# Streaming attention heads tiled by 55 queries over one 128-row key window each

## The chip, the core and the metric

The kernel runs on one core of a Trainium2 chip. The core has a matrix engine (TensorE, "PE" in the profile, with its weight loads as "PEld"), a vector engine (DVE), an activation engine (ACT), a general engine (POOL, which also issues software-described DMAs) and a queue engine (SP, which here issues plain and transposing DMAs). The metric is the device time of one execution in microseconds (us); lower is better.

## The reference, cut to what matters

Attention over 4 batches, 8 heads, 768 positions and head size 64, followed by a mixture of 4 experts over the 3072 rows of 512. Heads 0, 2 and 6 ("retrieval") attend to every earlier position. Heads 1, 3, 4, 5 and 7 ("streaming") see only the first 4 positions (the sinks) and the last 64.

```python
pos = np.arange(S)                        # S = 768
rel = pos[:, None] - pos[None, :]
causal = rel >= 0
is_sink = pos[None, :] < 4
in_win = (rel >= 0) & (rel < 64)
stream_keep = causal & (is_sink | in_win)
mask = np.where(retr, causal, stream_keep)            # per head
a = softmax(np.where(mask, q @ k.T / 8, -1e9))
x = (a @ v), heads side by side                       # (3072, 512)
...
for e in range(4):
    h = np.maximum(x @ w1[e], 0.0)                    # 512 -> 1024
    out += p[:, e:e+1] * (h @ w2[e])                  # 1024 -> 512
```

## The kernel before

**Groups.** The 768 positions of a batch are two chunks of 384 (`CH`), so there are eight groups `g` of (batch b, chunk c). The attention of a group makes `xT[g]`; `moe_group(g)` runs the four experts over its 384 rows. After the attention of group 0, the loop at the end runs `moe_group(g)` and, woven into it, `attention` of group g+1. Both are generators: a step of the expert work is four first-layer matmuls of 384 columns (line 648, then a relu on ACT into `hs`, line 661) or four second-layer matmuls of 512 columns (line 669). After each, attention steps are drawn until their nominal time has the share of `att_ns` that the expert work has of its stretch. So the order on every engine is fixed in the program[...].

**A head.** `scores` multiplies key tiles with the transposed queries into a bank of `pA` (four banks in all, shared with the first expert layer), takes the exp on ACT (line 499), and multiplies by a 0/1 mask on DVE (line 503) where the tile has an edge. `values` multiplies the value tiles with these into `pV` (two banks). A value tile of 128 columns holds the 64 of the head in one half and constants in the other, so that the same matmul gives the sum of the weights; ACT turns it into a reciprocal (Ln on line 548, Exp of the negative on line 558), and DVE scales (line 553). Heads interleave: `scores(h)` with `values(h-1)`.

**Tiles of a streaming head.** A key tile has 96 positions (`TK`) in its rows 32 to 127 and copies of the four sinks in rows 0 to 3. The 96 keys are visible to 160 queries (`TQ`), their own 96 and the next 64. A chunk therefore takes four tiles of 160, 160, 160 and 96 query columns, and chunk 1 also 64 columns of the last tile of chunk 0. `score_tiles` lists this: two banks and two masks a head.

**Data.** For groups 2 and later, POOL issues the loads two groups ahead (`load_k`, `load_q`, `load_v`), casting from float32 to float16. Keys and queries go to row-major buffers: `kRr` and `kSr` (one for each chunk), and `q16`. `dma_transposes`, issued from SP halfway through a group, copies the sinks into `kSr`, then transposes `q16`, `kRr` and `kSr` into `qT`, `kR` and `kS`. Values need no transposing; `sink_rows` copies their sinks. `kS` and `vS` exist twice, by the parity of the batch. Batch 0 is prepared on PE and DVE instead.

Of the kernel before, what the change touches and what calls it, by code (L numbers as in the profile page):

```python
# [10 lines left out]
FP16 = mybir.dt.float16  # L11
AF = mybir.ActivationFunctionType
ALU = mybir.AluOpType
# [4 lines left out]
def kernel(  # L18
# [21 lines left out]

    nc = tc.nc
    P = 128
    B, H, S, D = q.shape
# [19 lines left out]
    NT = S // TK  # L65
    TC = CH // TK
    assert NS <= R0 and NW == 64 and NS + NW <= TK

    pers = ctx.enter_context(tc.tile_pool(name="pers", bufs=1))
    att = ctx.enter_context(tc.tile_pool(name="att", bufs=1))  # L70
# [16 lines left out]
    w2sb = pers.tile([P, E * FTP, DM], FP16, name="w2sb")  # L87
    NR, NSH = len(RH), len(SH)
    kR = []
    kS = []  # L90
    vR = []
    vS = []
    for i in range(2):
        kR.append(pers.tile([P, NCH, NR, 3, P], FP16, name=f"kR{i}"))
        kS.append(pers.tile([P, NCH, TC, NSH, P], FP16, name=f"kS{i}"))
        vR.append(pers.tile([P, S // P, len(RH), P], FP16, name=f"vR{i}"))
        vS.append(pers.tile([P, NT, len(SH), P], FP16, name=f"vS{i}"))

    ident32 = pers.tile([P, P], FP32, name="ident32")
    ident16 = pers.tile([P, P], FP16, name="ident16")  # L100
# [3 lines left out]
    eps = pers.tile([P, 1], FP32, name="eps")  # L104
    mC = pers.tile([P, 2 * P], FP16, name="mC")
    mS = pers.tile([P, 4, TQ], FP16, name="mS")
    probs = pers.tile([P, NTILE, E], FP32, name="probs")
    psums = pers.tile([P, NTILE], FP32, name="psums")
    rprobs = pers.tile([P, NTILE], FP32, name="rprobs")
    p_sb = pers.tile([P, NTILE, E], FP32, name="p_sb")  # L110


    kRr = [pers.tile([P, NR, 3, P], FP16, name=f"kRr{c}") for c in range(NCH)]
    kSr = [pers.tile([P, TC, NSH, P], FP16, name=f"kSr{c}") for c in range(NCH)]


    def own(h):
        u = h % 2
        return slice(u * D, (u + 1) * D)

    def key_tile(b, h, t):

        i = b % 2
        if RETR[h]:
            return kR[i][:, t // 3, RH.index(h), t % 3, :]
        return kS[i][:, t // TC, t % TC, SH.index(h), :]

    def v_tile(b, h):

        i = b % 2  # L130
        if RETR[h]:
            return vR[i][:, :, RH.index(h), :]
        return vS[i][:, :, SH.index(h), :]


    q16 = {}
# [3 lines left out]

    def tiles_of(x, b, h, c):
        return x[b, h, c * CH : (c + 1) * CH, :].rearrange("(t r) d -> r t d", r=TK)

    def load_by_rows(x, x16, b, c):
        for j in range(3):
# [19 lines left out]
    def load_k(b, c):  # L165

        for h in range(H):
            if RETR[h]:
                gp.dma_start(  # L169
                    out=kRr[c][:, RH.index(h), :, own(h)], in_=rows_of(k, b, h, c)  # L170
                )
            else:
                gp.dma_start(  # L173
                    out=kSr[c][R0:P, :, SH.index(h), own(h)], in_=tiles_of(k, b, h, c)
                )

    qTs = {}
# [1 line left out]
    def alloc_qT(b, c):  # L179
        qTs[b, c] = att.tile([P, HP, CH], FP16, name="qT", bufs=2)  # L180

    def dma_transposes(b, c):
        i = b % 2
        first = kSr[0][R0 : R0 + NS, 0:1, :, :].rearrange("p t s x -> p t (s x)")
        nc.sync.dma_start(
            out=kSr[c][0:NS, :, :, :].rearrange("p t s x -> p t (s x)"),
            in_=first.to_broadcast([NS, TC, NSH * P]),
        )
        alloc_qT(b, c)
        for j in range(3):  # L190
            nc.sync.dma_start(
                out=qTs[b, c][:, :, j * P : (j + 1) * P],
                in_=q16[b, c][:, j, :, :].rearrange("p h d -> p (h d)"),
                transpose=True,
            )
        for x, xr in ((kR, kRr), (kS, kSr)):
            nc.sync.dma_start(
                out=x[i][:, c, :, :, :].rearrange("p t s x -> p (t s) x"),
                in_=xr[c].rearrange("p t s x -> p (t s x)"),
                transpose=True,  # L200
            )

    def load_v(b, c, heads):
        for h in heads:
            t = v_tile(b, h)
            if RETR[h]:
                gp.dma_start(  # L207
                    out=t[:, 3 * c : 3 * c + 3, own(h)], in_=rows_of(v, b, h, c)
                )
            else:  # L210
                gp.dma_start(  # L211
                    out=t[R0:P, TC * c : TC * (c + 1), own(h)],
                    in_=tiles_of(v, b, h, c),
                )

    def sink_row(b, h, c):
        t = v_tile(b, h)[:, :, own(h)]
        nc.vector.tensor_copy(  # L218
            out=t[0:NS, TC * c : TC * (c + 1), :],
            in_=t[R0 : R0 + NS, 0:1, :].to_broadcast([NS, TC, D]),  # L220
        )

    def sink_rows(b, c):
        x = vS[b % 2].rearrange("p t s x -> p t (s x)")
        nc.sync.dma_start(
            out=x[0:NS, TC * c : TC * (c + 1), :],
            in_=x[R0 : R0 + NS, 0:1, :].to_broadcast([NS, TC, NSH * P]),
        )
# [30 lines left out]
    def zero(eng, t):  # L259
        fill(eng, t.rearrange("p a b x -> p (a b x)"), 0.0)  # L260

    def one_values(eng, i, c):

        t = slice(3 * c, 3 * c + 3)
        fill(eng, vR[i][:, t, :, D:P], ONES)
        t = slice(TC * c, TC * (c + 1))
        fill(eng, vS[i][0:R0, t, :, :].rearrange("p t h x -> p t (h x)"), ONES)
        fill(eng, vS[i][:, t, 0:2, 0:D], ONES)
        fill(eng, vS[i][:, t, 2, D:P], ONES)
        fill(eng, vS[i][:, t, 3:5, 0:D], ONES)  # L270

    assert all(h % 2 == 0 for h in RH) and [h % 2 for h in SH] == [1, 1, 0, 1, 1]

# [18 lines left out]
    nc.vector.memset(eps, 1e-9)  # L292
    nc.vector.memset(ones, ONES)
    make_identity(nc, ident32)
    one_values(nc.vector, 0, 0)
    load_v(0, 0, [0, 1, 2, 3])
    zero(nc.vector, kR[0][:, 0, :, :, :])
    zero(nc.vector, kS[0][:, 0, :, :, :])
    nc.vector.tensor_copy(out=ident16, in_=ident32)


# [21 lines left out]
    def mask_s(x, n, keep, drop):  # L323
# [14 lines left out]
            fill=drop, base=-NW, pattern=[[1, TK]], channel_multiplier=-1,  # L338
        )

    mask_c(bC, 0.0, -60000.0)
    mask_s(bS, 3, 0.0, -60000.0)
    load_v(0, 0, [4, 5, 6, 7])
# [4 lines left out]
    load_triples(q, qt16, 0, 1)  # L348
    load_w2(0)
    zero(gp, kR[0][:, 1, :, :, :])  # L350
    zero(gp, kS[0][:, 1, :, :, :])
    one_values(gp, 0, 1)
    load_v(0, 1, range(5))
    load_w1(1, 0, F)
    load_v(0, 1, range(5, H))
# [3 lines left out]
        load_w2(e)  # L359
    mSf = mS.rearrange("p t x -> p (t x)")  # L360
    bSf = bS.rearrange("p t x -> p (t x)")


    xT = {}
# [4 lines left out]
    def attention(b, c):  # L369
# [5 lines left out]
        def transposes(hp):  # L375
            for x, is_k in ((k32 if first else k16, 1), (q32 if first else qt16, 0)):
# [20 lines left out]
                for u in range(2):  # L397
                    h = 2 * hp + u
                    r = slice(u * D, (u + 1) * D)
                    if RETR[h]:  # L400
                        nc.vector.tensor_copy(  # L401
                            out=rows_in_order(
                                kR[i][r, c, RH.index(h), :, :].rearrange(
                                    "r t x -> r (t x)"
                                )
                            ),
                            in_=cols(ps[r, :]),
                        )
                        continue
                    n = SH.index(h)  # L410
                    x_in, x_out = ps[r, 0:CH], kS[i][r, c, :, n, R0:P]
                    if first:
                        x_in = x_in.rearrange("r (t x) -> r t x", x=TK)
                    else:
                        x_in = x_in.rearrange("r (j t p) -> r j t p", j=3, t=TC)
                        x_out = x_out.rearrange("r t (p j) -> r j t p", j=3)
                    nc.vector.tensor_copy(out=x_out, in_=x_in)  # L417
                    sinks = kS[i][r, c, :, n, 0:NS]
                    if c == 0:
                        sink_k[h] = pers.tile([P, NS], FP16, name=f"sk{h}")  # L420
                        nc.vector.tensor_copy(out=sink_k[h][r, :], in_=ps[r, 0:NS])
                        src, op = ps[r, 0:NS], nc.vector.tensor_copy
                    else:
                        src, op = sink_k[h][r, :], nc.scalar.copy
                    src = src.rearrange("r (o x) -> r o x", o=1)
                    op(out=sinks, in_=src.to_broadcast([D, TC, NS]))
# [11 lines left out]
        def score_tiles(h):  # L438
            if RETR[h]:
                if c == 0:  # L440
# [7 lines left out]
                    (512, [(0, 0, 256, 128), (1, 128, 0, 384)], []),  # L448
                    (384, [(2, 0, 0, 384)], []),
                ]  # L450
            if c == 0:
                return [
                    (320, [(0, 0, 0, 160), (1, 160, 96, 160)], [(mSf, 0, 0, 320)]),
                    (256, [(2, 0, 192, 160), (3, 160, 288, 96)], [(mSf, 160, 0, 256)]),
                ]
# [18 lines left out]
        def scores(h):  # L474
            hp = h // 2
            es_of[h] = []
            for cols, parts, masks in score_tiles(h):
                ps = bank()
                ns = 0
                for n, (t, o, q0, nq) in enumerate(parts):  # L480
                    nc.tensor.matmul(  # L481
                        out=ps[:, o : o + nq],
                        lhsT=key_tile(b, h, t),
                        rhs=qTs[b, c][:, hp, q0 : q0 + nq],
                        start=(n == 0 or not first),
                        stop=not first,
# [26 lines left out]
        def values(h):  # L513
# [14 lines left out]
            for n, (es, t, o, q0, nq) in enumerate(work):  # L528
                nc.tensor.matmul(  # L529
                    out=ps[:, q0 : q0 + nq],  # L530
                    lhsT=v_tile(b, h)[:, t, :],
                    rhs=es[:, o : o + nq],
                    start=(n == 0),
                    stop=(n == len(work) - 1),
# [160 lines left out]
    for _ in attention(0, 0):  # L695
        pass

    for c in range(NCH):
        zero(gp, kRr[c])
        zero(gp, kSr[c])  # L700

    UNIT = FTP * DMP * mm_ns(CH) + 3 * FTP * mm_ns(DM)
    for g in range(G):
# [4 lines left out]
        if g + 2 < G:  # L708
            b2, c2 = divmod(g + 2, NCH)
            load_k(b2, c2)  # L710
            load_q(b2, c2)
            if b2 == 1:
                one_values(gp, b2, c2)
            load_v(b2, c2, range(H))

        begin = {0: 0.2, 1: 1.0}.get(g, 0.0) * UNIT
        end = {0: 2.2}.get(g, 0.93 * E) * UNIT

        att_ns = 4500.0 if nxt % NCH == 0 else 7700.0
        if nxt < NCH:  # L720
            att_ns += 8 * 3 * mm_ns(P)
        spent = 0.0
        done = 0.0
        to_transpose = g + 2 < G
# [47 lines left out]
```

The softmax here doesn't subtract the row's maximum and nothing guards it: scores larger than these inputs give would overflow.

## Time and profile before

The median of three runs is 417.66 us (417.56 to 418.54); the profiled execution spans 415.6 us.

| group of instructions | count | busy us | mean ns |
|---|---|---|---|
| PE first expert layer, 384 columns, L648 | 1024 | 187.7 | 326 |
| PE second expert layer, 512 columns, L669 | 768 | 180.7 | 379 |
| PE scores of streaming heads, 64 to 160 columns, L481 | 180 | 23.7 | 223 |
| PE scores of retrieval heads, 128 to 384 columns, L481 | 120 | 25.3 | 281 |
| ACT relu, L661 | 256 | 121.3 | 493 |
| ACT exp of scores, L499 | 152 | 71.6 | 481 |
| DVE masks of streaming heads, L503 | 70 | 22.2 | 317 |
| POOL issue of streaming key loads, L173 | 30 | 20.9 | 700 |
| POOL issue of streaming value loads, L211 | 40 | 28.1 | 706 |

Busy time is the time in which at least one instruction of the group was in flight. Matmuls are pipelined: each lasts longer than the distance to the next, so the mean duration of one isn't its cost. The granted clock of PE was 0.996 of full. DMA traffic is dense for the first third of the span and thin after it: in 40 slices, tenths of busy time were

```text
DMA  9999999999994700069963600046001000020002
```

### The profile page before, as it was taken

How to read it: one execution, taken by the hardware profiler on the slowest of the kernel's cores; microseconds unless marked ns; L12 is line 12 of the kernel's file. 1: busy time of each engine (PE TensorE's matmuls, PEld its weight loads, DVE VectorE, ACT ScalarE, POOL GpSimd, SP SyncE). 2: the span in 40 equal slices, each digit the busy share in tenths (PEclk: the TensorE clock that was granted, in tenths of full speed). 3: DMA queues.
4: the chain of work that ended last, by engine and by line, in shares of the span. 5: the costliest groups of instructions: out<-in, count | busy, mean ns of one | idle time of the engine just before them, and what ended most of it. 6: DMA issues, size and time to landing. Idle time of an engine off the chain costs nothing.

```text
span 415.6 us, 6541 instructions
## 1 busy us (share of the span) xinstructions
PE 401.6 (97%) x2520; PEld 228.3 (55%) x2520; DVE 163.3 (39%) x332; ACT 249.3 (60%) x539; POOL 120.2 (29%) x176
## 2 busy tenths in 40 slices
PE   7899999999999999999999999999999999999996
PEld 4665554555555555555555555555555555555552
DVE  7976553224432335333433333234443233432222
ACT  2676874337775657666764558666665577653331
POOL 8938319897980000039930000000000000000000
PEclk9899999999999999999999999999999999999999
DMA  9999999999994700069963600046001000020002
GB/s 173 146 196 204 209 205 109 177 182 146 88 91 118 98 1 2 25 126 164 83 39 94 117 2 2 0 107 105 2 0 61 18 2 0 2 76 2 0 0 76
DMA packets 117554, 33.70 MB, mean 81 GB/s; under 512 B 108100, under 2 KB 112404, under 8 KB 117524
## 3 DMA queue, kind: packets, MB, share of 16 engines
q0 software_dynamic: 71872, 17.05, 45.8%
q1 hardware_dynamic: 42452, 15.46, 18.1%
q10 hardware_dynamic: 3200, 0.79, 0.9%
q8 instruction: 19, 0.31, 0.3%
q14 instruction: 11, 0.09, 0.1%
HBM read 35.70 MB, written 6.29 MB: 101 GB/s over the span
## 4 chain that ended last, share of the span: by engine, by line
PE 86%; ACT 6%; DVE 4%; issue 1%; DMA 1%; ACTq 0%; DVEq 0%
PE pO L669 39%; PE pA L648 35%; PE pV L529 5%; PE pA L481 5%; ACT hs L661 2%; ACT rc L548 2%; DVE kS L417 1%; DMA q<-in_q_dram 1%; DVE vS L218 1%; ACT es L499 1%; ACT rc L558 1%; DVE kR L401 1%; ACTq L279 0%; DVE qT L392 0%; DVE es L503 0%
## 5 line engine op out<-in xcount | busy, mean ns | idle before, releaser
L648 PE MATMUL pA<-xT,w1sb 128*128 128x384 f16 x1024 | 187.7, 326 | 1.5 <-DVE kS L417 1.0
L669 PE MATMUL pO<-w2sb,hs 128*128 128x512 f16 x768 | 180.7, 379 | 0.0
L661 ACT ACTIVATE hs<-pA 128x384 f16<-128x384 f32 x256 | 121.3, 493 | 80.0 <-PE pA L648 73.4
L648 PEld LDWEIGHTS <-w1sb 128*128 128x128 f16 x1024 | 97.3, 98 | 59.7 <-issue 1.8
L669 PEld LDWEIGHTS <-hs 128*128 128x128 f16 x768 | 72.8, 98 | 72.7 <-ACT hs L661 0.5
L499 ACT ACTIVATE es<-pA 128x256 f16<-128x256 f32 (+3 forms) x152 | 71.6, 481 | 32.5 <-PE pA L481 29.5
L685 DVE SCALAR_TENSOR_TENSOR acc<-pO,p_sb,acc 128x512 f32<-128x512 f32 x72 | 54.0, 750 | 85.3 <-PE pO L669 84.8
L503 DVE TENSOR_TENSOR es<-es,mS 128x384 f16<-128x384 f16 (+1 forms) x70 | 22.2, 317 | 85.4 <-ACT es L499 85.0
L548 ACT ACTIVATE rc<-pV,eps 64x384 f32<-64x384 f32 x60 | 34.5, 575 | 34.7 <-PE pV L529 33.9
L173 POOL DMA_DIRECT2D kSr<-in_k_dram x30 | 20.9, 700 | 54.9 <-DMA kSr<-kSr 42.1
L553 DVE TENSOR_TENSOR xT<-pV,rc 64x384 f16<-64x384 f32 x60 | 33.1, 552 | 4.1 <-PE pA L648 1.7
L681 DVE TENSOR_SCALAR acc<-pO,p_sb 128x512 f32<-128x512 f32 x24 | 18.0, 750 | 37.7 <-PE pO L669 36.8
L558 ACT ACTIVATE rc<-rc 64x384 f32<-64x384 f32 x58 | 30.2, 522 | 1.8
L211 POOL DMA_DIRECT2D vS<-in_v_dram x40 | 28.1, 706 | 2.9 <-DMA q<-in_q_dram 2.2
L481 PE MATMUL pA<-qT,kS 128*128 128x160 f16 (+2 forms) x180 | 23.7, 223 | 3.4 <-ACT es L499 1.8
L481 PE MATMUL pA<-qT,kR 128*128 128x384 f16 (+2 forms) x120 | 25.3, 281 | 0.0
L481 PEld LDWEIGHTS <-kS 128*128 128x128 f16 x180 | 15.9, 98 | 15.2 <-issue 4.5
L503 DVE TENSOR_TENSOR es<-es,mC 128x256 f16<-128x256 f16 (+1 forms) x42 | 10.8, 256 | 29.4 <-ACT es L499 29.0
L529 PE MATMUL pV<-es,vR 128*128 128x384 f16 (+2 forms) x120 | 21.9, 281 | 0.0
L169 POOL DMA_DIRECT2D kRr<-in_k_dram x18 | 13.5, 751 | 21.4 <-issue 17.1
L207 POOL DMA_DIRECT2D vR<-in_v_dram x24 | 18.2, 759 | 4.5 <-DMA w2sb<-in_moe_w_dram 4.2
L529 PEld LDWEIGHTS <-vS 128*128 128x128 f16 x180 | 13.7, 98 | 9.8 <-issue 2.2
(68 smaller groups left out, 153.0 us busy)
## 6 DMA issues: line engine op xcount, KB each, us to landing
out_dram<-acc SPq DMA_DIRECT2D x24, 256.0 KB
w1sb<-in_moe_w_dram POOLq DMA_DIRECT2D x4, 1024.0 KB, 14.6
w2sb<-in_moe_w_dram POOLq DMA_DIRECT2D x4, 1024.0 KB, 17.6
q<-in_q_dram POOLq DMA_DIRECT2D x18, 128.0 KB, 4.8
vS<-in_v_dram POOLq DMA_DIRECT2D x40, 48.0 KB, 3.3
kSr<-in_k_dram POOLq DMA_DIRECT2D x30, 48.0 KB, 4.5
vR<-in_v_dram POOLq DMA_DIRECT2D x24, 48.0 KB, 3.4
kRr<-in_k_dram POOLq DMA_DIRECT2D x18, 48.0 KB, 4.6
```

What stands on the lines that cost most here:

```text
L211: gp.dma_start(out=t[R0:P, TC * c : TC * (c + 1), own(h)], in_=tiles_of(v, b, h, c),)
L481: nc.tensor.matmul(out=ps[:, o : o + nq], lhsT=key_tile(b, h, t), rhs=qTs[b, c][:, hp, q0 : q0 + nq], start=(n == 0 or not first), stop=no ...
L499: nc.scalar.activation(out=es[:, 0:cols], in_=ps[:, 0:cols], func=AF.Exp, scale=SC)
L503: nc.vector.tensor_tensor(out=es[:, o0:o1], in0=es[:, o0:o1], in1=m[:, mo : mo + o1 - o0], op=ALU.mult,)
L529: nc.tensor.matmul(out=ps[:, q0 : q0 + nq], lhsT=v_tile(b, h)[:, t, :], rhs=es[:, o : o + nq], start=(n == 0), stop=(n == len(work) - 1), ...
L548: nc.scalar.activation(out=rc[r, :], in_=ps[o, 0:CH], func=AF.Ln, bias=eps[o, :])
L553: nc.vector.tensor_tensor(out=xT[g][r, hp, :], in0=ps[r, 0:CH], in1=rc[r, :], op=ALU.mult)
L558: nc.scalar.activation(out=rc[r, :], in_=rc[r, :], func=AF.Exp, scale=-1.0)
L648: nc.tensor.matmul(out=pss[ft][:, 0:CH], lhsT=w1sb[:, e * DMP + ct, ft * P : (ft + 1) * P], rhs=xT[g][:, ct, :], start=(ct == 0), stop=(ct ...
L661: nc.scalar.activation(out=hs[:, ft, :], in_=ps[:, 0:CH], func=AF.Relu)
L669: nc.tensor.matmul(out=ps_o, lhsT=hs[:, ft, j * P : (j + 1) * P], rhs=w2sb[:, e * FTP + ft, :], start=(ft == 0), stop=(ft == FTP - 1),)
L685: nc.vector.scalar_tensor_tensor(out=acc[nt], in0=ps_o, scalar=p_ap, in1=acc[nt], op0=ALU.mult, op1=ALU.add,)
```

## The change

From batch 1 on, a streaming head is tiled by its queries instead of its keys. Each tile has 55 queries (`WQ`); the keys they can see, apart from the sinks, are 118 consecutive rows (`WK` = 55+64-1). A tile is loaded as the 128 rows that end at its last visible key, so neighbouring tiles overlap in the rows that they load, and the sinks are put over the first four rows. Seven tiles (`WT`) cover the 384 queries of a chunk; a tile no longer reaches into the next chunk. The aim is that each query column passes PE once for scores and once for values, in one bank with one exp and one mask.

With it come: one mask `mW` for all of these tiles, built on POOL after the zeroing of the key buffers; single instead of doubled `kRr` and `kSr`; the windows of chunk c live in the `kS` and `vS` buffer of index 1-c, whatever the batch; `put_sinks`, which keeps the sinks of chunk 0 for chunk 1 in `k_sinks` and `v_sinks`; smaller `att_ns`. Batch 0 keeps its tiles.

```diff
+    WQ = 55
+    WK = WQ + NW - 1
+    WT = 7
+    WO = P - WK + NW
...
+    def windows(x, c):
+        return x[1 - c][:, 0 : WT * NSH * P].rearrange(
+            "p (t s x) -> p t s x", t=WT, s=NSH
+        )
...
-    kRr = [pers.tile([P, NR, 3, P], FP16, name=f"kRr{c}") for c in range(NCH)]
-    kSr = [pers.tile([P, TC, NSH, P], FP16, name=f"kSr{c}") for c in range(NCH)]
+    kRr = pers.tile([P, NR, 3, P], FP16, name="kRr")
+    kSr = pers.tile([P, WT, NSH, P], FP16, name="kSr")
...
+    def windows_of(x, b, h, c):
+        first = ((b * H + h) * S + c * CH - WO) * D
+        return bass.AP(x.tensor, x.offset + first, [[D, P], [WQ * D, WT], [1, D]])
...
-                    out=kSr[c][R0:P, :, SH.index(h), own(h)], in_=tiles_of(k, b, h, c)
+                    out=kSr[:, :, SH.index(h), own(h)],
+                    in_=windows_of(k, b, h, c),
...
+    def put_sinks(x, sinks, c):
+        x = x.rearrange("p t s x -> p t (s x)")
+        src = sinks
+        if c == 0:
+            src = x[WO : WO + NS, 0:1, :]
+            nc.sync.dma_start(out=sinks, in_=src)
+        nc.sync.dma_start(
+            out=x[0:NS, :, :], in_=src.to_broadcast([NS, WT, NSH * P])
+        )
...
-        for x, xr in ((kR, kRr), (kS, kSr)):
+        for x, xr in ((kR[i][:, c, :, :, :], kRr), (windows(kSf, c), kSr)):
...
+            elif b:
+                gp.dma_start(
+                    out=t[:, :, own(h)], in_=windows_of(v, b, h, c)
+                )
...
+            if b:
+                starts = [max(WQ * t - 1, 0) for t in range(WT)] + [CH]
+                parts = [
+                    (t, q0, q0, q1 - q0)
+                    for t, (q0, q1) in enumerate(zip(starts, starts[1:]))
+                ]
+                return [(CH, parts, [(mWf, 1 + 2 * WQ * c, 0, CH)])]
...
-    for c in range(NCH):
-        zero(gp, kRr[c])
-        zero(gp, kSr[c])
+    zero(gp, kRr)
+    zero(gp, kSr)
+    mask_w()
...
-        att_ns = 4500.0 if nxt % NCH == 0 else 7700.0
+        att_ns = 3700.0 if nxt % NCH == 0 else 6600.0
         if nxt < NCH:
-            att_ns += 8 * 3 * mm_ns(P)
+            att_ns += 1100.0 + 8 * 3 * mm_ns(P)
```

## The prediction

> **What bounds the kernel now.** I read the busy table first, then the shares of the chain of waits, then the PE timeline.
>
> ```profile
> PE 401.6 (97%) x2520; PEld 228.3 (55%) x2520; DVE 163.3 (39%) x332; ACT 249.3 (60%) x539; POOL 120.2 (29%) x176
> PE 86%; ACT 6%; DVE 4%; issue 1%; DMA 1%; ACTq 0%; DVEq 0%
> ```
>
> TensorE (PE) is busy 97% of the span and carries 86% of the chain that ends last; in the middle of the run it is never starved for long (the windows view: PE busy 276.99 us of the 279.00 us from 91 to 370). So a matmul column taken away is worth its time; ACT and DVE work taken away counts only where PE waits for it.
>
> Busy times of matmuls overlap (326 ns each, yet eight 384-column ones fill 1.30 us), so I price by start to start. Timeline of PE, columns start, length, line, shape of the first, count:
>
> ```profile
> 107.53 0.41 PE L529 MATMUL pV<-es,vS 128*128 128x160 f16 x4
> 107.78 1.46 PE L648 MATMUL pA<-xT,w1sb 128*128 128x384 f16 x8
> ...
> 151.92 0.33 PE L481 MATMUL pA<-qT,kS 128*128 128x64 f16 x3
> 152.08 1.46 PE L648 MATMUL pA<-xT,w1sb 128*128 128x384 f16 x8
> 153.38 0.44 PE L529 MATMUL pV<-es,vS 128*128 128x64 f16 x5
> 153.66 1.46 PE L648 MATMUL pA<-xT,w1sb 128*128 128x384 f16 x8
> 154.96 0.28 PE L481 MATMUL pA<-qT,kS 128*128 128x160 f16 x2
> 155.07 0.81 PE L648 MATMUL pA<-xT,w1sb 128*128 128x384 f16 x4
> ```
>
> Four streaming matmuls of one head in chunk 0 (160+160+160+96 columns) take 107.78-107.53 = 0.25 us; the five of chunk 1 (64 more) 0.28 us. A pair 160+96 takes 0.11, so a 160 takes (0.25-0.11)/2 = 0.07, a 96 0.04, and the 64 in the run of three 0.16-0.14 = 0.02 to 0.03. The trace's own stamps say 69, 42 and 28 ns, each with a weight load of its own.
>
> PE's few waits in batches 1 to 3 are of two kinds:
>
> ```profile
> 122.09 0.30 PE L529 MATMUL pV<-es,vS 128*128 128x160 f16 x2
> 122.62 0.27 PE L529 MATMUL pV<-es,vS 128*128 128x160 f16 x2 [0.23 <-DVE es L503]
> ...
> 156.24 0.33 PE L481 MATMUL pA<-qT,kS 128*128 128x64 f16 x3 [0.35 <-ACT hs L661]
> ```
>
> The first, once for each attention of chunk 0: the last head's values come right behind its second score tile, and the third matmul waits for that tile's exp and mask. It should start 0.14 after the first and starts 0.53 after: 0.39 lost, and by the stamps 0.44 at 218.2 and 314.7, 1.28 us in all. The second, once for each attention of chunk 1: a streaming score tile wants a bank of pA that ACT has not read yet; 0.52 lost there and 0.22 just after, 2.2 us for three attentions.
>
> **What the Trainium skill says.** (1) TensorE: Matmul & The Clock Gate, section "Wait — 56ns, not 53.3ns?": a warm matmul of N columns costs N/2.4 plus about 2.5 ns, never under about 25 ns start to start. The trace agrees for the large ones (162 ns for 384); its smallest is 28 ns for 64 columns. (2) The same page, "Back-to-back issue gap", puts a sustained stream of weight load and 128-column matmul at about 81 ns. The trace disagrees: two such in a row (from 151.80 to 151.92) are 56 ns each. (3) Whether a mask read from an odd element keeps DVE's two-per-cycle rate: VectorE: DVE Perf Modes ("Mode 2×_1P") asks for 4-byte alignment, Vector Engine (DVE) Microarchitecture Reference ("5.1 Performance modes") says that alignment makes no difference. No mask in this trace starts at an odd element, so neither is shown.
>
> **The change part by part.**
>
> *PE.* Thirty streaming attentions of a head (5 heads, 3 batches, 2 chunks: 15 of each chunk). Each has two runs, scores and values. Before: 249 ns a run in chunk 0 (3x69+42), 277 in chunk 1 (28 more). After: seven matmuls of 54 or 55 columns, 384 in all and none computed twice. The unknown is their spacing when seven weight loads follow each other. A straight line through 64, 96, 128 and 160 columns (28, 42, 56, 69) gives 24 at 55; the page's floor is 25; the smallest shown is 28. I take 26, ends 25 and 28. A run is then 182 ns: 67 saved in chunk 0, 95 in chunk 1, 30 runs of each: 30x67 + 30x95 = 4.9 us. Ends: 5.3 (at 25) and 4.0 (at 28). The batch-0 attentions keep their 96-key tiles: nothing there.
>
> *ACT and DVE.* The exps of a streaming head go from 320+256 columns (434+383 ns) or 384+256 (493+383) to one of 384 (493); the masks from 326+290 or 358+290 to one of 358, or, at half rate because of the odd start, some 560 (the slope between 256 and 384 columns, 0.53 ns a column, doubled). ACT loses 15x324 + 15x383 = 10.6 us and DVE about 8 (or 2), none of it on the path except where PE waits. The order of the changed program puts 28 moe matmuls and the last three of head 6 between head 7's scores and its values in chunk 0, about 5 us, where four stood before: exp plus mask (0.49+0.36, or 0.56) fit in. I count all 1.28 us. In chunk 1 the crowded first-layer stretch holds two streaming score tiles where it held four; but PE also passes it faster. I count 0.5 of the 2.2, ends 0 and 2.2.
>
> *Loads.* Each streaming k or v load grows from 96x4 to 128x7 rows of 64: 384 to 896 packets, 60 loads, 30,720 packets more. The software queue spent 45.8% of 16 engines' span on 71,872 packets: 2.65 ns a packet over all engines, so 6.8 us for five loads. The k transpose grows from 20 blocks to 35; the longest of before took 5.22 us, 0.26 a block, 3.9 more. The tight case is the first, chunk 0 of batch 1:
>
> ```profile
> 63.28 0.72 POOL L173 DMA_DIRECT2D kSr<-in_k_dram  x1 [4.35 <-DMA w2sb<-in_moe_w_dram]
> 63.99 2.66 POOL L147 DMA_DIRECT2D q<-in_q_dram  x3
> ...
> 74.40 5.22 SPq L197 DMA_TRANSPOSE kS<-kSr  x1
> ...
> 82.22 0.68 SPq L225 DMA_DIRECT2D vS<-vS  x1
> ```
>
> POOL is held there by the landing of w2, so the extra masks and zeroes on POOL (mW: nine short operations, like the bS ones of 0.26 to 0.60 us, some 3.5 us; one memset of kSr fewer) hide behind that wait. kS would be transposed by 79.62+6.8+3.9 = 90.3; its first use is at 93.98. The sinks of v, issued at 82.22, slip to 92.9 and a second copy of 0.65 goes with them; first use 99.97. It fits, with 3.7 us the smallest room.
>
> *Waits added.* kRr and kSr are single now: POOL's loads for chunk 1 wait until chunk 0 is transposed, and q and v loads stand behind them on POOL's queue. From 90.3: eight k loads at 0.72 to 0.87 (97), landing at some 100, q at 105, three q transposes, kR and kS (35 blocks) until 119. The first use of kR is at 127.70, of kS at 132.42. Later groups have 42 us or more from one to the next. Values of batch b+1 wait for attention of batch b in the same chunk, three groups before they are read. SP carries two sink copies where it had one. I cost all of it at nothing: PE's first-layer and second-layer matmuls hide it.
>
> *Pace.* The new att_ns only spread the shorter attention over the same stretch; no time of its own.
>
> Sum: 4.9 + 1.28 + 0.5 = 6.7 us off, 417.66 - 6.7 = 411.0.
>
> **The rivals.**
>
> A. The matmuls shrink, but ACT's backlog merely moves: in the streaming stretch each head still has its Ln, Exp and scale (575+522 on ACT, 552 on DVE), now for less PE time. For it: the page's ACT waits sit exactly there. Against it: fewer tiles want a bank. Then 4.0 to 4.9 remain: 417.66 - 4.4 = 413.3.
>
> B. Small matmuls in a row are bound by their weight loads. Each load lasts 98 ns in the profile, and no two matmuls under 96 columns stand together in the streaming work, so 28 could be the luck of a load prefetched beside a long matmul. If the 56 of the 128-column pairs is the spacing of a load, a run takes 392 ns: 30x143 + 30x115 = 7.7 us more; with 1.8 us of waits gone, 423.6: slower. It breaks even at 249/7 to 277/7, about 37 ns. Against it: the load of the 160 behind the 64 was issued in that same 28 ns.
>
> C. The first streaming data of batch 1 come late. DMA is 9 tenths busy in that stretch (slices 6 to 12) and the loads share it with the transposes; if both take half again as long (16 instead of 10.7 us), kS is there at 95.7 and v's sinks at some 98 to 101, and the chunk behind it also slips. PE then waits some 2 to 5 us in this program's fixed order: 417.66 - 6.7 + 5 = 416.0.
>
> **How the numbers follow.** The forecast 0.50, A 0.26, B 0.12, C 0.12. Predicted: 411.0. The lowest end takes 5.3 + 1.28 + 2.2 = 8.8 off: 408.9. B alone is left out above, so the range goes from 409.0 to C's 416.0. Faster by over 0.3% (below 416.4): the forecast, A, and most of C: 0.84. Within 0.3%: 0.04. Slower: B, 0.12.
>
> **What would show it.** Runs of seven on PE should be 0.18 us from the first start to that of the next group; at 0.26 or more B holds. The wait of L529 for DVE's es at the end of each chunk-0 attention should be gone. ACT's busy time should fall by about 10 us, DVE's by 2 to 8 (the new mask's duration, 358 or 560, tells which page is right). A PE wait near 94 to 101 us for kS or vS shows C. I am wrong if the spacing is above 37 ns, or if new PE waits of over 6 us appear.

## The result and the profile after

The changed kernel takes 414.79 us (median of four runs, 413.08 to 414.84) against 417.71: a ratio of 0.9916 with a 95% interval of 0.9888 to 0.9945. That is 2.9 us faster where 6.7 were forecast. The time lies inside the range of 409.0 to 416.0, nearer to rival A (413.3) than to the forecast (411.0).

The times of every kernel here lie mostly near two values some 1.7 us apart, which part ahead of group 1 and so ahead of the changed attention; so below I set the lower times beside each other (before 415.88, changed 413.06), or count inside one trace from the start of group 1 on.

The busy table of the changed kernel, and the shares of its chain of waits:

```profile
PE 395.8 (96%) x2670; PEld 222.4 (54%) x2670; DVE 155.8 (38%) x302; ACT 240.9 (58%) x509; POOL 141.7 (34%) x176
PE 86%; ACT 6%; DVE 4%; DMA 2%; issue 1%; ACTq 0%; DVEq 0%
```

PE is busy 5.8 us less, ACT 8.4 and DVE 7.5 less, and the chain looks as it did: nothing new bounds the kernel. But 2.2 of PE's 5.8 us lie in the first 24 us, long ahead of the changed attention. From the start of group 1 to that of group 7 PE is busy 283.60 us instead of 287.24, and idle 2.9 instead of 2.0. The longest wait in that part is in the first-layer stretch of a chunk-1 attention, the counterpart of the wait at 156.24 before. PE timeline of the changed kernel (start, length, engine, line, shape of the first, count, and the wait ahead):

```profile
153.64 0.36 PE L561 MATMUL pA<-qT,kS 128*128 128x54 f16 x7
153.84 0.81 PE L728 MATMUL pA<-xT,w1sb 128*128 128x384 f16 x4
154.49 0.36 PE L609 MATMUL pV<-es,vS 128*128 128x54 f16 x7
154.69 1.46 PE L728 MATMUL pA<-xT,w1sb 128*128 128x384 f16 x8
155.98 0.36 PE L561 MATMUL pA<-qT,kS 128*128 128x54 f16 x7
156.18 0.81 PE L728 MATMUL pA<-xT,w1sb 128*128 128x384 f16 x4
157.72 0.81 PE L728 MATMUL pA<-xT,w1sb 128*128 128x384 f16 x4 [0.73 <-ACT hs L741]
```

Two readings. A run of seven takes 153.84-153.64 = 0.20 us; the stamps say 28 ns for each of them. And the last four first-layer matmuls start 1.54 us after the four before them, where 0.65 is due: 0.9 lost for a bank of pA. ACT in the same stretch:

```profile
156.03 0.57 ACT L628 ACTIVATE rc<-pV,eps 64x384 f32<-64x384 f32 x1
156.64 0.52 ACT L638 ACTIVATE rc<-rc 64x384 f32<-64x384 f32 x1
157.18 0.87 ACT L741 ACTIVATE hs<-pA 128x384 f16<-128x384 f32 x2
```

ACT has no gap there: it takes the Ln and Exp of one streaming head, then the relu that frees the bank.

I summed the distances between matmul starts group by group, and took as waiting what exceeds columns/2.4 + 2.5 ns by more than 8 ns (the spacing formula is the one that the prediction quotes):

| us | before | changed | relus of 2, 4, 6 on DVE | two banks | relus of 0 to 6 on DVE |
|---|---|---|---|---|---|
| streaming matmuls, groups 1 to 6 | 15.87 | 11.87 | 11.87 | 11.71 | 11.87 |
| waits of groups 1, 3, 5 | 1.47 | 0.78 | 0.78 | 2.21 | 0.0 |
| waits of groups 2, 4, 6 | 2.20 | 4.35 | 1.23 | 6.21 | 1.22 |
| start of group 1 to start of group 7 | 289.26 | 286.52 | 283.39 | 289.63 | 282.62 |

(Group g weaves in the attention of group g+1: 1, 3 and 5 that of chunk 0, 2, 4 and 6 that of chunk 1.)

### The profile page after: what moved, and what is told of

It is laid out like the page before. It is cut to its first block, busy times and chain, and to the rows that moved or that the text cites. A ratio compares the mean times of both kernels' runs of the same rounds, so it can differ in the third digit from the quotient of the medians.

```text
span 413.1 us, 6801 instructions
## 1 busy us (share of the span) xinstructions
PE 395.8 (96%) x2670; PEld 222.4 (54%) x2670; DVE 155.8 (38%) x302; ACT 240.9 (58%) x509; POOL 141.7 (34%) x176
## 3 DMA queue, kind: packets, MB, share of 16 engines
q0 software_dynamic: 102592, 20.98, 59.5%
## 4 chain that ended last, share of the span: by engine, by line
PE 86%; ACT 6%; DVE 4%; DMA 2%; issue 1%; ACTq 0%; DVEq 0%
PE pO L749 40%; PE pA L728 36%; PE pV L609 5%; PE pA L561 4%; ACT hs L741 2%; DMA q<-in_q_dram 2%; ACT rc L628 2%; DVE kS L490 1%; ACT rc L638 1%; DVE vS L261 1%; ACT es L579 1%; DVE kR L474 1%; DVE qT L465 0%; PE pO L355 0%; PE pV L355 0%
## 5 line engine op out<-in xcount | busy, mean ns | idle before, releaser
L579 ACT ACTIVATE es<-pA 128x512 f16<-128x512 f32 (+3 forms) x122 | 61.0, 511 | 22.7 <-PE pA L561 20.9
L204 POOL DMA_DIRECT2D kSr<-in_k_dram x30 | 30.1, 1006 | 36.5 <-issue 14.7
L250 POOL DMA_DIRECT2D vS<-in_v_dram x30 | 30.4, 1024 | 34.8 <-PE pV L609 34.0
L583 DVE TENSOR_TENSOR es<-es,mW 128x384 f16<-128x384 f16 x30 | 10.8, 360 | 57.2 <-ACT es L579 57.2
L246 POOL DMA_DIRECT2D vR<-in_v_dram x24 | 19.2, 800 | 4.3 <-DMA w2sb<-in_moe_w_dram 4.2
L561 PEld LDWEIGHTS <-kS 128*128 128x128 f16 x255 | 13.9, 98 | 9.5 <-issue 2.9
L561 PE MATMUL pA<-qT,kS 128*128 128x55 f16 (+4 forms) x255 | 16.6, 195 | 2.2 <-ACT es L579 1.6
```

The lines of the kernel that those rows point to most:

```text
L204: gp.dma_start(out=kSr[:, :, SH.index(h), own(h)], in_=windows_of(k, b, h, c),)
L250: gp.dma_start(out=t[:, :, own(h)], in_=windows_of(v, b, h, c))
L561: nc.tensor.matmul(out=ps[:, o : o + nq], lhsT=key_tile(b, c, h, t), rhs=qTs[b, c][:, hp, q0 : q0 + nq], start=(n == 0 or not first), stop ...
L579: nc.scalar.activation(out=es[:, 0:cols], in_=ps[:, 0:cols], func=AF.Exp, scale=SC)
```

## The experiments

Two theories are set against each other. T: the matmuls save 4.0 us and the ends of the chunk-0 attentions 0.7, and PE's waits for ACT in the chunk-1 attentions give 2.2 back. R, the rival: the small gain has another cause, and these waits an accident, or fixed by the order, or not ACT's.

**The changed kernel again.**

> The changed kernel once more, beside the others. Theory T (matmuls of 54 and 55 columns are 28 ns apart, which saves 4.05 us, and PE's waits for ACT in the three chunk-1 attentions, 1.45 us each where they were 0.73, give 2.2 of it back): 414.8, some 2.9 below the kernel before. Rival R (the saving is small for another reason and the waits are an accident of the profiled execution): the same time, but the waits of 1.45 us are not there again in the profile.

Measured: 413.06 us median (413.02 to 414.93), before 417.60 (415.88 to 419.19), ratio 0.9916 (0.989 to 0.9942). The waits of groups 2, 4 and 6 were 1.46 us each, as in the first trace. Lower times 2.8 apart. The waits are no accident of one execution: they belong to the program.

**Three of eight relus to DVE in groups 2, 4 and 6.** In `moe_group`, for the changed kernel and for the one before:

```diff
-                    nc.scalar.activation(
-                        out=hs[:, ft, :], in_=ps[:, 0:CH], func=AF.Relu
-                    )
+                    if g in (2, 4, 6) and ft in (1, 4, 6):
+                        nc.vector.tensor_scalar(
+                            out=hs[:, ft, :], in0=ps[:, 0:CH], scalar1=0.0,
+                            scalar2=None, op0=ALU.max,
+                        )
+                    else:
+                        nc.scalar.activation(...)
```

> The changed kernel with three of eight relus of the expert layer in groups 2, 4 and 6 moved from ACT to DVE, so that ACT has 1.5 us less in each first-layer stretch. Theory T: the waits of PE in these groups fall from 1.45 us to 0.4 or less each, some 3.2 us in all: 411.6. Rival R (PE waits for the fixed order, for pV banks or for es, not for ACT's throughput): 414 or more.

> The kernel before with the same three of eight relus on DVE in groups 2, 4 and 6. Theory T: its waits in these groups fall from 0.73 to 0.2 or less each, 1.6 us in all: 416.1, so that the changed tiles with the same relus are 4.5 to 4.8 us faster than this one (4.05 on the matmuls, 0.7 at the ends of the chunk-0 attentions). Rival R: 417.5, and the two differ by 2.9 as before.

Measured: the changed kernel with these relus takes 411.64 (409.91 to 411.70), ratio 0.9851 (0.9823 to 0.9879); the kernel before with them 416.22 (414.51 to 417.26), ratio 0.9963 (0.9949 to 0.9978). The waits of groups 2, 4 and 6 fell from 1.45 to 0.41 each in the one, and from 0.73 to 0.36 in the other. Lower times: 3.15 off the changed kernel, 1.37 off the one before, so that the two now differ by 4.6 instead of 2.8. The same stretch of the changed kernel with these relus, PE timeline:

```profile
155.73 0.36 PE L561 MATMUL pA<-qT,kS 128*128 128x54 f16 x7
155.93 1.46 PE L728 MATMUL pA<-xT,w1sb 128*128 128x384 f16 x8
157.22 0.36 PE L609 MATMUL pV<-es,vS 128*128 128x54 f16 x7
```

The eight first-layer matmuls run through in 1.29 us; the order on PE is that of the changed kernel, only ACT's work is less. So it is ACT that PE waited for, and this had taken 1.8 us of what the tiles bring. What was left over is a little more than T said (0.4 and 0.2). R falls in so far as it says that the waits are not ACT's; that the order decides when ACT's work comes is not excluded by this run.

**The pace of before.**

```diff
-        att_ns = 3700.0 if nxt % NCH == 0 else 6600.0
+        att_ns = 4500.0 if nxt % NCH == 0 else 7700.0
         if nxt < NCH:
-            att_ns += 1100.0 + 8 * 3 * mm_ns(P)
+            att_ns += 8 * 3 * mm_ns(P)
```

> The changed kernel with the pace numbers of before (att_ns 4500 and 7700, no 1100 for the group ahead of batch 1). The attention is woven in faster; in chunk 1 the first-layer stretch of the third expert then holds one streaming and two retrieval score tiles and up to three Ln and Exp pairs, more ACT work than now. Theory T: PE's waits in groups 2, 4 and 6 change with it, up by 0.3 to 1 us each: 415.5 to 418. Rival R (pace and place of the attention steps do not matter): 414.8.

Measured: 412.93 (412.90 to 414.94), ratio 0.9913 (0.9887 to 0.994). A miss for T's number; the time itself fits R (no effect). But the waits moved (0.28 us at 154.1, 0.75 at 157.0, 0.52 at 168.9 in group 2 where there had been 0.29, 0.27 and 0.90 at other places), but their sum rose by 0.09 a group only, and the 0.22 us of groups 3 and 5 vanished. So counting ACT's work in one stretch by hand says where PE may wait, not how long. The new pace numbers of the change are worth nothing, which is what the prediction said of them.

**The one exp undone.** Same matmuls, but each streaming score tile over two banks:

```diff
-                return [(CH, parts, [(mWf, 1 + 2 * WQ * c, 0, CH)])]
+                m0 = 1 + 2 * WQ * c
+                n0 = starts[4]
+                late = [(t, o - n0, q0, nq) for t, o, q0, nq in parts[4:]]
+                return [
+                    (n0, parts[:4], [(mWf, m0, 0, n0)]),
+                    (CH - n0, late, [(mWf, m0 + n0, 0, CH - n0)]),
+                ]
```

> The changed kernel with each streaming score tile split again over two banks, two exps and two masks (four parts of 220 columns, three of 164); the matmuls are the same. It undoes the one-exp part of the change alone. Exps of 220 and 164 columns should take some 350 and 300 ns where one of 384 takes 491. Theory T (ACT's backlog decides PE's waits): 0.16 us more ACT work a head and one more bank, so the waits of the chunk-1 attentions grow from 1.46 us by 0.3 to 1 each; and head 7's values stand four matmuls behind its second tile again, so about 0.5 us comes back at the end of each chunk-0 attention. In all 2.4 to 4.5 us slower than the changed kernel, that is level with the kernel before or up to 1.5 above or 0.5 below it. Rival R (the one exp is worth nothing, PE's columns are all): 2.8 below the kernel before, as the changed kernel is.

Measured: 418.29 (416.52 to 418.49), ratio 1.0005 (0.9986 to 1.0023): level with the kernel before. Lower times: 3.5 above the changed kernel; from the start of group 1 to that of group 7 the traces show 3.1. Groups of ACT (count, busy us, mean ns), then PE, of this kernel:

```profile
L585 ACT ACTIVATE es<-pA 128x219 f16<-128x219 f32 x30 | 10.6, 355 | 2.9 <-PE pA L567 2.9
L585 ACT ACTIVATE es<-pA 128x165 f16<-128x165 f32 x30 | 9.3, 310 | 25.1 <-PE pA L567 25.1
```

```profile
157.68 0.81 PE L734 MATMUL pA<-xT,w1sb 128*128 128x384 f16 x4 [1.13 <-ACT hs L747]
...
218.08 0.27 PE L615 MATMUL pV<-es,vS 128*128 128x54 f16 x4
218.92 0.24 PE L615 MATMUL pV<-es,vS 128*128 128x55 f16 x3 [0.57 <-DVE es L589]
```

355+310 = 665 ns of exp where one takes 491. The wait for ACT grew from 0.9 to 1.3 us, and the wait of the values for their mask at the end of a chunk-0 attention is back in groups 3 and 5 (0.84 us from start to start where 0.11 is due). By the table, some 4 us less of matmuls than in the kernel before bought nothing without the single exp: the waits rose by 4.75. Two cautions. The split gives the weave (the fixed interleaving of attention and expert steps) one more step a head, so the order on PE shifts with it, and this run doesn't tell the two apart. And ACT is busy 245.4 us in all here, less than the 249.3 of the kernel before, whose waits in groups 2, 4 and 6 were 2.20 us and not 6.21: the sum of ACT's work does not set them.

**Narrower parts.**

```diff
-                starts = [max(WQ * t - 1, 0) for t in range(WT)] + [CH]
+                starts = [40 * t for t in range(WT)] + [CH]
```

> The changed kernel with the seven parts of a streaming head cut at 40, 80, 120, 160, 200 and 240 columns, so six of 40 and one of 144 (the last tile's keys do not cover its queries: part of the scores are of the wrong keys). All starts are even. Theory F (a matmul with a fresh weight load cannot follow the last in under 28 ns): the six of 40 are 28 ns apart, the 144 takes 62, a run 230 ns where seven of 55 take 196, so about 60 x 0.034 = 2.0 us slower than the changed kernel. Rival G (28 ns comes from the odd starts of the 55-column parts, or is the price of 55 columns): 19 to 25 ns apart, a run 180 to 212, within 1 us of the changed kernel.

Measured: 414.71 (413.83 to 415.57), ratio 0.9938 (0.9916 to 0.996), lower times 0.8 above the changed kernel. PE timeline:

```profile
113.87 0.38 PE L609 MATMUL pV<-es,vS 128*128 128x40 f16 x7
114.09 1.46 PE L728 MATMUL pA<-xT,w1sb 128*128 128x384 f16 x8
```

A run takes 0.22 us; by the stamps 25 or 26 ns for each of the first five parts of 40, 28 or 29 for the sixth, ahead of the 144, and 61 or 62 for the 144. F falls: matmuls with a fresh weight load each do follow one another in less than 28 ns. Nor is it the odd start that makes 28: the first part of the 55-column tiling, 54 columns from column 0, takes 28 too. What is shown is 25 ns at 40 columns and 28 at 54, 55 and 64; why 54 costs as much as 64, and the sixth 40 more than the others, stays open.

**The relus of groups 0 to 6 on DVE**, that is `if g < G - 1 and ft in (1, 4, 6)`, and the same with the pace of before:

> The changed kernel with three of eight relus on DVE in groups 0 to 6, not in 2, 4 and 6 alone. Theory T: the waits that are left in groups 1, 3 and 5 (0.34, 0.22, 0.22) and 2, 4, 6 (0.41 each with these relus) are ACT's too in the former: some 0.6 us less than with the relus in groups 2, 4 and 6; 6.5 below the kernel before, 411.1. Rival R (DVE becomes the late one, since it also has the acc of the second layer and the scales): no gain over that kernel, or a loss.

> The last kernel with the pace numbers of before (att_ns 4500 and 7700) as well. The pace took the waits of groups 3 and 5 from 0.22 to nothing and left those of 2, 4 and 6 at 1.54. Theory T: with ACT relieved the latter fall to 0.4 or less and the former stay at nothing: 6.5 to 7 below the kernel before, about 410.8. Rival R (the waits at the old pace are of another kind, not ACT's): 1.54 stays, 3 below the kernel before.

Measured: 410.80 (409.08 to 410.86), ratio 0.9838 (0.9811 to 0.9865), for the first; 410.14 (410.12 to 411.85), ratio 0.9838 (0.9811 to 0.9864), for the second. Lower times 409.08 and 410.12: 6.8 and 5.8 below the kernel before. In both, groups 1, 3 and 5 have no wait left; in groups 2, 4 and 6 the first keeps 0.41 and the second 0.76 each, more than T expected of it. Of these 0.76 us, 0.64 are a wait for a relu on DVE (at 154.94 us in group 2): there R was right that DVE becomes the late one. The first is the fastest version here and beats both kernels. Its busy table:

```profile
PE 394.7 (96%) x2670; PEld 222.3 (54%) x2670; DVE 199.1 (49%) x386; ACT 208.3 (51%) x425; POOL 141.8 (35%) x176
```

ACT and DVE now carry about the same.

## Why the prediction was right or wrong, point by point

**What bounds the kernel: right.** PE still carries 86% of the chain, and its columns were worth their time once ACT let PE pass: 4.6 us apart with the relus moved, where the matmuls and the ends of chunk 0 account for 4.0 + 0.7.

**The matmul term: right in kind, its size at the low end.** 26 ns was taken, 28 came, the end of 4.0 us that was kept for the range. The straight line through the trace's spacings (24 ns at 55 columns) failed below 64 columns. Rival B (56 ns, 423.6 us) is refuted by the spacing itself. In the Trainium skill, TensorE: Matmul & The Clock Gate, section "Back-to-back issue gap", gives about 81 ns for a weight load with a 128-column matmul; this does not hold here, where such a pair takes 56 ns, and one of 40 to 64 columns 25 to 28. The floor of about 25 ns in the same page's section "Wait — 56ns, not 53.3ns?" does hold: 25 at 40 columns. Its formula for larger N, 25.4 ns at 55 columns, is too low there.

**The end of chunk 0: right in mechanism, 0.7 of the 1.28.** PE's waits for es in the values of groups 1, 3 and 5 are gone from the profile, and came back in 3 and 5 when the exp was split. But the prediction did not count that other waits could take their place: 0.34, 0.22 and 0.22 us in the first-layer stretches of these groups, where some 0.2 in all had been. They too vanished with the relus on DVE.

**The chunk-1 term: this is the step that failed.** "I count 0.5 of the 2.2, ends 0 and 2.2" stood for a gain; the waits doubled instead, from 2.20 to 4.35 us. The count of score tiles in the stretch was right (two instead of four), but counting was not enough. In this stretch ACT was busy 6.65 of 6.88 us before (152.08 to 158.96) and 5.82 of 6.99 after (151.58 to 158.57): less work and a smaller share, and yet PE waited 0.90 us in it instead of 0.73. "PE also passes it faster" was hardly so: 6.09 against 6.15 us without the waits. What the traces do show to differ is when ACT's work comes. The values of one retrieval head stood just ahead of the first-layer stretch and now stand eight first-layer matmuls inside it, and their Ln and Exp (575+522 ns) with them. Before:

```profile
151.80 0.28 PE L529 MATMUL pV<-es,vR 128*128 128x128 f16 x2
152.12 0.58 ACT L548 ACTIVATE rc<-pV,eps 64x384 f32<-64x384 f32 x1 [2.70 <-PE pV L529]
```

After:

```profile
151.58 1.46 PE L728 MATMUL pA<-xT,w1sb 128*128 128x384 f16 x8
152.88 0.28 PE L609 MATMUL pV<-es,vR 128*128 128x128 f16 x2
153.60 0.58 ACT L628 ACTIVATE rc<-pV,eps 64x384 f32<-64x384 f32 x1
```

In the first-layer stretch before that one ACT now takes two such pairs where it took one, and PE waits 0.56 us there where it did not wait. Groups 4 and 6 show the same. That PE waits for ACT is shown by the relus on DVE. That the moved pairs make the waits longer is a reading of the traces: no run moved such a pair alone, and with the pace of before the waits moved while their sum stayed, so what sets their size stays open. Rival A named the right engine, and the waits ahead of the change stood in that stretch; but A priced the backlog as no gain, and it was a loss of 2.15 us, and its "less PE time" is not what these stretches show. With 4.0 and 0.7 gained, the sum is some 2.6; from the start of group 1 to that of group 7 the trace shows 2.74. Against the terms of the forecast (4.9, 1.28 and 0.5) that is 0.9, 0.6 and 2.65 us short. That the time still lies inside the range is in part luck: this term fell outside its own ends, and what left room for it was rival C's end of the range, though C did not come about.

**ACT and DVE: right.** The exps alone fell by the 10.6 us worked out (71.6 to 61.0), and DVE's busy time by 7.5. ACT's busy time fell by 8.4 only, since its instructions now overlap less (their durations sum to 10.7 us less). The mask that starts at an odd element:

```profile
L583 DVE TENSOR_TENSOR es<-es,mW 128x384 f16<-128x384 f16 x30 | 10.8, 360 | 57.2 <-ACT es L579 57.2
```

360 ns, as against 358 for an even start. In the Trainium skill, Vector Engine (DVE) Microarchitecture Reference, section "5.1 Performance modes", which says that alignment makes no difference, agrees with the trace; the 4-byte alignment that VectorE: DVE Perf Modes asks for ("Mode 2×_1P") is not needed in this instruction.

**The loads: right that they hide.** From group 1 on no wait of PE in the changed kernel is put down to a DMA. The software queue's packets rose to 102,592, by the 30,720 worked out. POOL's issue of a streaming load was dearer than the 0.87 us taken, but stayed hidden. The group of POOL, and the two early k transposes on SP's queue:

```profile
L204 POOL DMA_DIRECT2D kSr<-in_k_dram x30 | 30.1, 1006 | 36.5 <-issue 14.7
```

```profile
75.27 9.41 SPq L236 DMA_TRANSPOSE kS<-kSr  x1
...
103.87 8.37 SPq L236 DMA_TRANSPOSE kS<-kSr  x1
```

The first ends at 84.7, where 90.3 was estimated, and is first used at 94.1; the second at 112.2, where 119 was. The estimate added 6.8 us for the packets of k, but those loads were queued early behind w2, and their last landed at 67.6, only 1.8 later than before. Rival C did not come about: PE has no wait near 94 to 101 us. The single kRr and kSr do hold POOL up (12.6 us of waits for the kS transposes from group 1 on), but nothing on PE waits for that; doubled buffers beside these tiles were not run.

## What to carry to other kernels

When PE is the bound and another engine drains its banks, the drain engine's share of a stretch does not say whether PE will wait: here ACT's share fell from 97 to 83% and PE's wait grew. Follow in the trace where the drains that do not shrink (here Ln and Exp) come between those that PE needs next (here relu), and expect the weave to move them when its steps get shorter. Merging two drains into one, with the change of order that comes with it, can be worth almost as much as the columns: here 3.1 us by the traces against 4.0. A drain that two engines can do is a cheap lever; three of eight relus on DVE gave another 4.0 us.

## What the runs showed of the hardware that was not expected

- Matmuls with a fresh 128-column weight load each follow one another at 25 ns for 40 columns and 28 ns for 54, 55 and 64, where the straight line through 64 to 160 columns gave 24 at 55.
- A DVE mask of 384 fp16 columns from an odd element took 360 ns, from an even one 358.
- POOL's issue of a load took 0.70 us for 384 rows of 64 and 1.01 us for 896.
